# A transform kernel's first batch: folds on VectorE in a new order, half-rate samples as one narrow tile, masked copies a step ahead

## The chip, the cores and the metric

The kernel runs on one core of a Trainium2 chip. A core has TensorE (PE in the profile; PEld is its weight load), VectorE (DVE), ScalarE (ACT), GpSimd (POOL) and SyncE (SP, which only issues loads and stores here), each with its own stream of instructions, joined by semaphores. The metric is the device time of one execution in microseconds, as the median of several runs.

## What is computed

The input x is 4 x 3072 x 256. Three parts follow one another:

```python
X = np.fft.fft(np.fft.fft(x, axis=1), axis=2).real                     # attention
h = np.maximum(X @ w_in, 0.0); u, v = h[..., :512], h[..., 512:]       # moe
v_n = (v - mean(v)) / np.sqrt(var(v) + 1e-6)                           # over the last axis
v_s = np.einsum('ts,bsd->btd', w_spatial, v_n) + b_spatial[None, :, None]
y = (u * v_s) @ w_out
out = (sigmoid(y @ w_gate) * (y @ w_val)) @ w_out2                     # moe2, on 12288 rows
```

w_in is 256 x 1024, w_spatial 3072 x 3072. Where a product needs more than one pass's accuracy, a number is kept as a high and a low part (`h` and `l` at a name's end) and the product is three matmuls (`mm3`).

## The kernel before

The real part of the two-dimensional transform is symmetric, so that the sequence is folded (sums and differences of mirrored quarters, `folds`) before it is multiplied by cosine tables. A batch has three fold tiles `fo` (m = 0, 1, 2), each made from two half loads `xt` (`fold_x`, twelve two-input operations on a half), and split into `fh` and `fl` (`split_fold`; tile 2 first swaps some rows between partition halves by four ScalarE copies, `exchange`). The second axis, of 256, is folded into w_in: `first_weights` multiplies w_in, decoded from 64-bit words by `convert` into `wih` and `wil`, by `fd` into `gh`, `gl` and `g3`, once for all batches.

Two sets of samples stand outside of this scheme. The half-rate samples (column 128 of the 256, one value for a token and batch) are loaded as `xn`, three tiles of 128x1024, folded, split into `fohl` and multiplied by the same tables into `nts`; the copy `nt` of one unit is masked for one batch by ScalarE. The special samples `xs` (five slots of 128 columns) become `sps`, weighted by `spc` in some products.

The prologue makes all of this for batch 0 and the weights. It ends at about 70 us with the first `psv`. Then the main stage runs until about 346 us: 4 batches, each with four units (3, 2, 0, 1), each of eight or seven blocks: `v_block` (a product `psv` of 128 tokens by 512, of which half is mirrored: `ev`, `tv`) and `u_block` (`psu`, `eu`, `tu`). The order in which a block's parts are issued is written out by `put_off`: the first part in its step, the second (`second`, which reads the finished sum from its bank once by ScalarE and once by VectorE, `mirror`) `LAG` steps later, the third (relu and statistics, or the store) one step after that. Layer normalization of a unit (`ln1`, `root`, `ln2`, `norms`) follows some steps later. Folds and splits of the next batch are put into steps by a table (`plan`), on GpSimd. From 346 us on TensorE works through the products of w_spatial and what follows; nothing there is touched.

There is no scheduler: each engine does its instructions in the order in which the code issues them. Loads on SP's queue and on GpSimd's go out in their order on each; a load into a ring's buffer waits for the last reader of what was in it. The tables `c1`, `c2`, `c3`, `spc` and `fd` are loaded by GpSimd, the rest by SP.

Of the kernel before, what the change touches and what calls it, by code (L numbers as in the profile page):

```python
# [156 lines left out]
def layouts(x, moe_w_in, moe_w_spatial, moe_b_spatial, moe_w_out, moe2_w_gate, moe2_w_val, moe2_w_out):  # L157
# [14 lines left out]
    n = np.zeros((3, P, 8, P), np.float32)  # L172
    gn = g[..., D // 2].reshape(B, 3, P, 8)
    for b in range(B):
        for c in range(3):
            n[..., 32 * b + c] = gn[b]
# [3 lines left out]
    for at in (0, 32, 64):  # L180
# [9 lines left out]
        "xn": n,  # L190
# [48 lines left out]
def tile_kernel(ctx: ExitStack, tc: tile.TileContext, t: dict, out: bass.AP):  # L239
# [151 lines left out]
    def fft(fold, b, unit, q, e=0, ps=None):  # L391
# [49 lines left out]
    def convert(two):  # L441
        new = lambda: tmp.tile([P, 512], F32, tag="cv", name="cv", bufs=5)
        values = from64_rest(from64_first([words[i] for i in two], new), new())
        for i, value in zip(two, values):
            c, h = pieces[i]
            sl = slice(h * 512, h * 512 + 512)
            split(wih[0][:, c, sl], wih[1][:, c, sl], value)
# [9 lines left out]
    fold0(nc.vector, 0, 0)  # L457
    xts[2, 0] = load_x(0, 2, 0)
    fold0(nc.gpsimd, 1, 0)
    fd = tmp.tile([P, 2 * 512 + 256], F32R, name="fd")  # L460
    nc.gpsimd.dma_start(fd, t["fd"])
    fold0(nc.vector, 0, 1)
    words.append(load_w(2))
    xts[2, 1] = load_x(0, 2, 1)
    fold0(nc.gpsimd, 1, 1)
    load_table(cst, "c3", {"c3p": (3, R3), "c3q": (3, H)})
    nc.gpsimd.dma_start(spc, t["spc"])
    convert([0, 1])
    words.append(load_w(3))
    nc.sync.dma_start(masks, t["masks"])  # L470
    xs = tmp.tile([P, B + 1, 2, P], F32, name="xs")
    nc.sync.dma_start(xs, t["xs"])
    xns = []

    def load_xn(m):
        xn = tmp.tile([P, 8, P], F32, tag="xt", name="xn", bufs=RING)
        nc.sync.dma_start(xn, t["xn"][m])
        xns.append(xn)

    load_xn(0)  # L480
    load_xn(1)
    fold = [split_fold(fo[0], 0)]
    fold0(nc.vector, 2, 0)
# [12 lines left out]
    def first_weights(h):
# [8 lines left out]
        for a, ps in enumerate(sums):  # L505
            nc.scalar.copy(gc[0][:, a, sl], ps)
            nc.vector.tensor_tensor(out=gc[1][:, a, sl], in0=ps, in1=f(gc[0][:, a, sl]), op=ALU.subtract)
        ps = ps_w.tile([P, 512], F32, tag="pa", name="psg3")
        for c in range(2):
# [3 lines left out]
        nc.scalar.copy(g3[:, sl], ps)  # L513
        nc.vector.scalar_tensor_tensor(
            out=g3[:, sl], in0=f(g3[:, sl]), scalar=masks[:, 1:2], in1=ps, op0=ALU.mult, op1=ALU.add
        )

    first_weights(1)

    fold_n = []  # L520

    def fold_nyquist(eng, m):
        folds(eng, [(0, xns[m], xns[m][:, 4:8, :])])

    def split_nyquist(m):
# [18 lines left out]
    split_nyquist(2)
# [10 lines left out]

# [3 lines left out]
    up = pool(r0, "up", 3, "right")  # L559

    def unit_blocks(pq, b, unit):
# [20 lines left out]
        def v_block(m):  # L582
# [31 lines left out]
        def u_block(fb):  # L614
# [32 lines left out]
        def ln2():  # L647
# [709 lines left out]
```

## Time and profile before

| what | value |
|---|---|
| median of 3 runs | 2972.27 us (2971.44 to 2974.28) |
| the profiled execution | 2973.02 us, its span 2971.2 us |
| granted TensorE clock over the span | 0.990 |
| busy over the span | PE 2867.2, DVE 2064.7, ACT 1323.5, POOL 401.2 us |
| PE by 40 slices of 74 us, in tenths | 3 in the first, 8 in the next four, 9 in the rest |
| chain that ended last, share of the span | PE 87%, DVE 8%, ACT 2%, issue 2%, DMA 1% |
| q1 (SP) over the span | 143712 packets, 442.70 MB |
| q0 (GpSimd) over the span | 2320 packets, 14.82 MB |

Times of rows count from the start of the span. In a timeline row the first number is the start, the second the duration (of all of them, where a row ends in x2), and in brackets stands how long the engine was idle before it and what released it. Rows of one line and shape that follow one another are put together.

### The profile page before, as it was taken

How to read it: one execution, taken by the hardware profiler on the slowest of the kernel's cores; microseconds unless marked ns; L12 is line 12 of the kernel's file. 1: busy time of each engine (PE TensorE's matmuls, PEld its weight loads, DVE VectorE, ACT ScalarE, POOL GpSimd, SP SyncE). 2: the span in 40 equal slices, each digit the busy share in tenths (PEclk: the TensorE clock that was granted, in tenths of full speed). 3: DMA queues.
4: the chain of work that ended last, by engine and by line, in shares of the span. 5: the costliest groups of instructions: out<-in, count | busy, mean ns of one | idle time of the engine just before them, and what ended most of it. 6: DMA issues, size and time to landing. Idle time of an engine off the chain costs nothing.

```text
span 2971.2 us, 34046 instructions
## 1 busy us (share of the span) xinstructions
PE 2867.2 (96%) x12550; PEld 2359.4 (79%) x12550; DVE 2064.7 (69%) x2908; ACT 1323.5 (45%) x2117; POOL 401.2 (14%) x408
## 2 busy tenths in 40 slices
PE   3888899999999999999999999999999999999999
PEld 2777788888878888888887888788888888888887
DVE  8898875768765765576666476866666666766665
ACT  3777532323232232332223233655555555555554
POOL 5774121122111002111002010000000000000000
PEclk8999999999999999999999999999999999999999
DMA  6565875778765776776876474200000000000000
GB/s 230 187 235 221 313 276 196 278 244 316 264 221 175 260 252 211 242 257 222 282 259 223 154 271 166 84 29 29 29 10 20 29 29 29 15 15 29 29 15 15
DMA packets 149656, 472.28 MB, mean 159 GB/s; under 512 B 16624, under 2 KB 18160, under 8 KB 149104
## 3 DMA queue, kind: packets, MB, share of 16 engines
q1 hardware_dynamic: 143712, 442.70, 43.2%
q0 software_dynamic: 2320, 14.82, 1.3%
q10 hardware_dynamic: 3456, 12.58, 1.1%
q8 instruction: 98, 1.61, 0.2%
q14 instruction: 70, 0.57, 0.1%
HBM read 387.46 MB, written 82.58 MB: 158 GB/s over the span
## 4 chain that ended last, share of the span: by engine, by line
PE 87%; DVE 8%; ACT 2%; issue 2%; DMA 1%; ACTq 0%; DVEq 0%; SPq 0%
PE bank L261 28%; PE bank L262 28%; PE bank L260 28%; DVE stats L610 1%; DVE gl L994 1%; DVE g L986 1%; ACT wh L751 1%; DVE st L747 1%; DVE tv L580 0%; DVE wl L754 0%; DVE tu L580 0%; DMA v_d<-tv 0%; PE psv L588 0%; DVE tv L659 0%; PE psf L260 0%
## 5 line engine op out<-in xcount | busy, mean ns | idle before, releaser
L262 PE MATMUL bank<-wh,vl 128*128 128x512 f32 x2016 | 786.3, 390 | 0.0
L261 PE MATMUL bank<-wl,vh 128*128 128x512 f32 x2016 | 786.0, 390 | 0.0
L260 PE MATMUL bank<-wh,vh 128*128 128x512 f32 x2016 | 785.4, 390 | 0.0
L754 DVE TENSOR_TENSOR wl<-st,wh 128x1024 fp32r<-128x1024 f32 x252 | 331.4, 1315 | 390.9 <-ACT wh L751 388.9
L751 ACT CAST wh<-st 128x1024 fp32r<-128x1024 f32 x252 | 265.2, 1053 | 594.6 <-PE bank L262 351.6
L260 PEld LDWEIGHTS bank<-wh,vh 128*128 128x128 f32 x2016 | 379.3, 188 | 79.9
L261 PEld LDWEIGHTS bank<-wl,vh 128*128 128x128 f32 x2016 | 379.1, 188 | 80.0
L262 PEld LDWEIGHTS bank<-wh,vl 128*128 128x128 f32 x2016 | 378.9, 188 | 79.0
L1240 DVE TENSOR_TENSOR t<-t,bank 128x512 f32<-128x512 f32 x144 | 99.0, 688 | 250.3 <-PE bank L262 250.2
L747 POOL TENSOR_TENSOR st<-st 128x1024 f32<-128x1024 f32 x60 | 156.5, 2608 | 812.9 <-DMA st<-v_d 512.2
L261 PE MATMUL bank<-x,wgh 128*128 128x512 f32 x673 | 265.9, 395 | 0.0
L262 PE MATMUL bank<-x,wgl 128*128 128x512 f32 x673 | 265.5, 395 | 0.0
L260 PE MATMUL bank<-x,wgh 128*128 128x512 f32 x673 | 264.1, 392 | 0.4 <-ACT t L1252 0.4
L747 DVE TENSOR_TENSOR st<-st 128x1024 f32<-128x1024 f32 x180 | 226.1, 1256 | 53.9 <-DMA st<-in_wt 53.9
L1261 DVE TENSOR_TENSOR gl<-s,gh 128x512 fp32r<-128x512 f32 x288 | 199.4, 693 | 57.4 <-ACT gh L1259 44.5
L262 PE MATMUL bank<-gh,wv 128*128 128x512 f32 x576 | 227.6, 395 | 0.0
L260 PE MATMUL bank<-gh,wv 128*128 128x512 f32 x576 | 226.8, 394 | 0.8 <-ACT gh L1254 0.8
L261 PE MATMUL bank<-gl,wv 128*128 128x512 f32 x576 | 225.8, 392 | 0.2 <-DVE gl L1261 0.2
L1231 ACT ACTIVATE s<-s 128x512 f32<-128x512 f32 x144 | 91.0, 632 | 149.0 <-DVE s L1230 149.0
L260 PEld LDWEIGHTS bank<-x,wgh 128*128 128x128 f32 x673 | 126.4, 188 | 31.2 <-ACT t L1252 0.8
L261 PEld LDWEIGHTS bank<-x,wgh 128*128 128x128 f32 x673 | 126.3, 188 | 30.6
L262 PEld LDWEIGHTS bank<-x,wgl 128*128 128x128 f32 x673 | 126.2, 188 | 28.6
(233 smaller groups left out, 4564.2 us busy)
## 6 DMA issues: line engine op xcount, KB each, us to landing
st<-in_wt SPq DMA_DIRECT2D x432, 512.0 KB, 5.3
st<-v_d SPq DMA_DIRECT2D x144, 512.0 KB, 4.9
u<-u_d SPq DMA_DIRECT2D x96, 256.0 KB, 4.4
u_d<-tu SPq DMA_DIRECT2D x56, 384.0 KB, 3.1
v_d<-tv SPq DMA_DIRECT2D x80, 256.0 KB, 2.5
xt<-in_xh SPq DMA_DIRECT2D x24, 512.0 KB, 4.6
x_d<-x ACTq DMA_DIRECT2D x24, 512.0 KB, 3.2
raw<-x_d SPq DMA_DIRECT2D x24, 512.0 KB, 4.5
```

Of the source, the lines that this page charges most:

```text
L260: nc.tensor.matmul(out=ps, lhsT=w[0], rhs=x[0], start=first, stop=False, **kw)
L261: nc.tensor.matmul(out=ps, lhsT=w[0], rhs=x[1], start=False, stop=False, **kw)
L262: nc.tensor.matmul(out=ps, lhsT=w[1], rhs=x[0], start=False, stop=last, **kw)
L610: nc.vector.bn_stats(stats[:, sg * 3 + m, :], tiles[sg * 3 + m])
L747: (nc.gpsimd if kind == "v" else nc.vector).tensor_tensor(out=tiles[0], in0=tiles[0], in1=tiles[1], op=ALU.add if sign > 0 else ALU.subtract)
L751: nc.scalar.copy(hl[0], tiles[0])
L754: lows.append(lambda: nc.vector.tensor_tensor(out=hl[1], in0=tiles[0], in1=f(hl[0]), op=ALU.subtract))
L986: nc.vector.scalar_tensor_tensor(out=g, in0=side["u"][d], scalar=0.0, in1=g, op0=ALU.max, op1=ALU.mult)
L994: side["low"] = lambda: nc.vector.tensor_tensor(out=gl, in0=g, in1=f(gh), op=ALU.subtract)
L1231: nc.scalar.activation(s1, s1, AF.Sigmoid)
L1240: nc.vector.tensor_tensor(out=g["t2"], in0=g["t2"], in1=g["b"], op=ALU.add)
L1261: nc.vector.tensor_tensor(out=l, in0=s, in1=f(h), op=ALU.subtract)
```

## The change

Six things are different.

- All six half folds of batch 0 are on VectorE; three of them were on GpSimd. Conversion of the words, the `wil` halves, the folds and the weights' second parts are issued in a new order.
- The half-rate samples of all batches and tiles are one tile of 128 x 8 x 12, folded once on VectorE (48 columns and fewer) and spread to the places of `fohl`, three columns for a batch, when they are split; the rest of `fohl` is set to zero by GpSimd.
- GpSimd's loads of `c3`, `spc` and `c2` stand right after that of `fd`.
- The special samples are mirrored in two parts, two slots before the first product and three after the half-rate products.
- In the main stage VectorE's `mirror` is issued ahead of ScalarE's copy of the same bank, and the masked copy `nt` of the following unit is issued in the step of a unit's last block (`own_samples`).
- `ln2` has four operations on the root instead of five.

```diff
-    def fold0(eng, m, hd):
-        fold_x(eng, xts[m, hd], fo[m], hd, new_et(tmp if eng is nc.gpsimd else xp))
+    def fold0(m, hd):
+        fold_x(nc.vector, xts[m, hd], fo[m], hd, new_et())
 
     xts[0, 0] = load_x(0, 0, 0)
-    xts[1, 0] = load_x(0, 1, 0)
     xts[0, 1] = load_x(0, 0, 1, tmp, RING)
     words = [load_w(0), load_w(1)]
+    xts[1, 0] = load_x(0, 1, 0)
     xts[1, 1] = load_x(0, 1, 1, tmp, RING)
...
+    nc.sync.dma_start(masks, t["masks"])
+    xn = tmp.tile([P, 8, 3 * B], F32, name="xn")
+    nc.sync.dma_start(xn, t["xn"])
...
     load_table(cst, "c3", {"c3p": (3, R3), "c3q": (3, H)})
     nc.gpsimd.dma_start(spc, t["spc"])
...
+    fold0(0, 0)
+    fold0(0, 1)
+
+    fn = tmp.tile([P, 4, 3 * B], F32, name="fn")
+    folds(nc.vector, [(0, xn, fn)])
+    exchange(fn[:64, 1, 2 * B :], fn[64:, 0, 2 * B :])
+    xts[2, 0] = load_x(0, 2, 0)
+    xts[2, 1] = load_x(0, 2, 1, tmp, RING)
+    rest = convert([0, 1])
+    words += [load_w(2), load_w(3)]
     load_table(cst, "c2", {"c2p": (3, H), "c2q": (3, H)})
...
+    fold0(1, 0)
+    rest()
...
+    take = first_weights(1)
+    fold0(1, 1)
...
+    mirror_samples(slice(0, B + 1, B))
+    fold = [split_fold(fo[0], 0)]
+    take()
+    rest = convert([2, 3])
+    fold0(2, 0)
+    rest()
+    take = first_weights(0)
+    fold0(2, 1)
+    fold.append(split_fold(fo[1], 1))
...
+    for m in range(3):
         if m == 2:
-            exchange(xns[m][:64, 5, :], xns[m][64:, 4, :])
+            fold.append(split_fold(fo[2], 2))
         hl = fop.tile([P, 2, 4, P], F32R, tag="fo", name="fohl")
-        split(hl[:, 0], hl[:, 1], xns[m][:, 4:8, :])
+        nc.gpsimd.memset(f(hl), 0.0)
+        hi, lo = (hl[:, i].rearrange("p s (b k) -> p s b k", k=32)[:, :, :, 0:3] for i in range(2))
+        src = fn[:, :, m * B : m * B + B].unsqueeze(3).to_broadcast([P, 4, B, 3])
+        nc.scalar.copy(hi, src)
+        nc.vector.tensor_tensor(out=lo, in0=src, in1=f(hi), op=ALU.subtract)
         fold_n.append((hl[:, 0:1], hl[:, 1:2]))
...
+    mirror_samples(slice(1, B))
...
+    def own_samples(b, unit):
+        nt = stp.tile([P, R3], F32R, tag="nt", name="nt", bufs=1)[:, : R3 if unit == 3 else H]
+        nc.scalar.activation(nt, f(nts[unit]), AF.Identity, scale=masks[:, 3 + b : 4 + b])
+        nt_of[b, unit] = nt
...
+                mirror(tiles[3 + m], ev, ps)
                 nc.scalar.activation(tiles[m], ps, AF.Relu)
-                mirror(tiles[3 + m], ev, ps)
...
+                mirror(tu[:, 1, :], eu[:, :H], ps[:, :H])
                 nc.scalar.copy(tu[:, 0, :], ps[:, :H])
-                mirror(tu[:, 1, :], eu[:, :H], ps[:, :H])
...
-            nc.vector.tensor_tensor(out=sd[:, a], in0=y[:, a], in1=y[:, a], op=ALU.mult)
-            nc.vector.tensor_tensor(out=sd[:, a], in0=sd[:, a], in1=ve[:, a], op=ALU.mult)
-            nc.vector.tensor_scalar(out=sd[:, a], in0=sd[:, a], scalar1=-0.5, scalar2=1.5, op0=ALU.mult, op1=ALU.add)
-            nc.vector.tensor_tensor(out=y[:, a], in0=y[:, a], in1=sd[:, a], op=ALU.mult)
+            stt(out=ve[:, a], in0=y[:, a], scalar=-0.5, in1=ve[:, a], op0=ALU.mult, op1=ALU.mult)
+            nc.vector.tensor_tensor(out=ve[:, a], in0=ve[:, a], in1=y[:, a], op=ALU.mult)
+            stt(out=y[:, a], in0=ve[:, a], scalar=1.5, in1=y[:, a], op0=ALU.add, op1=ALU.mult)
...
-            put_off(step, block)
+            put_off(step, block, follows if block is blocks[-1] else None)
```

First place, the loads at the start. SP's queue before, from its first load (`xt` are the halves of batch 0, `words` those of w_in):

```order
L366 DMA xt<-in_xh 128x1024 x3
L265 DMA words<-in_w_in 128x1024 x2
L366 DMA xt<-in_xh 128x1024 x2
L265 DMA words<-in_w_in 128x1024
L366 DMA xt<-in_xh 128x1024
L265 DMA words<-in_w_in 128x1024
L470 DMA masks<-in_masks 128x7
L472 DMA xs<-in_xs 128x1280
L477 DMA xn<-in_xn 128x1024 x3
```

and now, up to the first loads of the next batch:

```order
L362 DMA xt<-in_xh 128x1024 x2
L261 DMA words<-in_w_in 128x1024 x2
L362 DMA xt<-in_xh 128x1024 x2
L467 DMA masks<-in_masks 128x7
L469 DMA xn<-in_xn 128x96
L471 DMA xs<-in_xs 128x1280
L362 DMA xt<-in_xh 128x1024 x2
L261 DMA words<-in_w_in 128x1024 x2
L362 DMA xt<-in_xh 128x1024 x3
```

GpSimd's stream now begins, after its constants, with four loads; of before it had twelve fold operations ahead of `fd`, twelve more ahead of `c3` and `spc`, and a third half ahead of `c2`:

```order
L466 DMA fd<-in_fd 128x1280
L326 DMA c_167<-in_c 128x4620
L473 DMA spc<-in_spc 128x1538
L326 DMA c_238<-in_c 128x4608
L544 MEMSET fohl 128x1024 [waits DVE_49] x3
L326 DMA c_434<-in_c 128x4608
```

`xn` is now one narrow load in the eighth place of SP's queue (two, two, two and the masks stand ahead), and 128x1280 to 128x4608 of tables are issued by GpSimd beside it; the memsets of `fohl` wait for VectorE.

Second place, ScalarE in the prologue, from its first instruction to the weights. Before:

```order
L276 ACT_TABLE_LOAD
L276 ACTIVATE cv<-words 128x512
L277 ACTIVATE cv<-words 128x512
L276 ACTIVATE cv<-words 128x512
L277 ACTIVATE cv<-words 128x512
L255 CAST wih<-cv 128x512 x2
L255 CAST fh<-fo 128x1024
L491 CAST sps<-es 128x5x128
L491 CAST sps<-xs 128x5x128
L506 CAST gh<-psg 128x512 x2
L513 CAST g_133<-psg_314 128x512
```

and now:

```order
L341 COPY ex<-fn 64x4
L342 COPY ex<-fn 64x4
L343 COPY fn<-ex 64x4
L344 COPY fn<-ex 64x4
L272 ACTIVATE cv<-words 128x512
L273 ACTIVATE cv<-words 128x512
L272 ACTIVATE cv<-words 128x512
L273 ACTIVATE cv<-words 128x512
L448 CAST wih<-cv 128x512 x2
L524 CAST sps<-es 128x2x128
L524 CAST sps<-xs 128x2x128
L251 CAST fh<-fo 128x1024
```

Four exchange copies of `fn`, which VectorE writes after the fold of `xn`, stand ahead of the first words, and the cast `fh` stands behind those of the samples.

Third place, ScalarE at the first change of units in the main stage (batch 0, from unit 3 to unit 2), with what each instruction waits for. Before:

```order
L622 COPY eu<-psu 128x386 [waits PE_49,Activation_49]
L628 COPY tu<-psu 128x384 [waits PE_49]
L608 ACTIVATE tv<-tv 128x512 [waits DVE_49]
L570 ACTIVATE nt<-nt_136,masks 128x384
L595 COPY ev<-psv 128x512 [waits PE_49]
L622 COPY eu<-psu 128x384 [waits PE_49,Activation_49]
L628 COPY tu<-psu 128x384 [waits DMAHW2_49,PE_49]
```

and now:

```order
L637 COPY eu<-psu 128x386 [waits PE_49,Activation_49]
L576 ACTIVATE nt<-nt_136,masks 128x384
L644 COPY tu<-psu 128x384 [waits DVE_49]
L623 ACTIVATE tv<-tv 128x512
L610 COPY ev<-psv 128x512 [waits PE_49]
L637 COPY eu<-psu 128x384 [waits PE_49,Activation_49]
L644 COPY tu<-psu 128x384 [waits DMAHW0_49,DVE_49]
```

`nt` of the next unit has moved ahead of `tu` and `tv`'s relu, and `tu`, which waited for TensorE, now waits for VectorE's `mirror`; VectorE's own wait on ScalarE at that place is gone, and its second statistic waits for the relu.

## Rows read from the trace of the kernel before

**Rows 1.** Windows of the main stage: start:end, length, busy time by engine, clock, DMA.
```profile
100.00:280.00 180.00, 151.95 (x722) 134.96 (x721) 163.75 (x368) 131.94 (x267) 124.14 (x180) 0.94 0.62 222
```

**Rows 2.** Waits of PE, 70 to 346 us: total, times, longest.
```profile
PE psv L588 <- ACT nt L570: 34.3, 16, 6.3
```

**Rows 3.** Waits of DVE, 70 to 346 us.
```profile
DVE tv L580 <- ACT tv L602: 19.0, 11, 3.4
DVE tu L580 <- ACT tu L628: 9.2, 13, 1.5
```

**Rows 4.** Timeline of DVE, 0 to 72 us: start, duration, operation, wait before.
```profile
4.63 0.69 DVE L371 TENSOR_TENSOR et<-xt 128x512 f32<-128x512 f32 x1 [4.63 <-DMA xt<-in_xh]
...
20.83 1.02 DVE L282 TENSOR_SCALAR cv<-cv 128x512 f32<-128x512 f32 x2
...
27.32 3.29 DVE L256 TENSOR_TENSOR wil<-cv,wih 128x512 fp32r<-128x512 f32 x2
...
32.20 1.21 DVE L371 TENSOR_TENSOR et<-xt 128x512 f32<-128x512 f32 x1
...
37.38 0.21 DVE L362 TENSOR_TENSOR fo<-xt 128x64 f32<-128x64 f32 x1
...
42.70 1.27 DVE L507 TENSOR_TENSOR gl<-psg,gh 128x512 fp32r<-128x512 f32 x2
...
44.56 1.34 DVE L282 TENSOR_SCALAR cv<-cv 128x512 f32<-128x512 f32 x2
...
52.42 1.29 DVE L256 TENSOR_TENSOR wil<-cv,wih 128x512 fp32r<-128x512 f32 x2
...
56.80 1.23 DVE L256 TENSOR_TENSOR fl<-fo,fh 128x1024 fp32r<-128x1024 f32 x1 [1.60 <-ACT fh L255]
...
60.40 1.53 DVE L354 TENSOR_TENSOR xn<-xn 128x512 f32<-128x512 f32 x1
...
63.90 0.28 DVE L362 TENSOR_TENSOR xn<-xn 128x128 f32<-128x128 f32 x1
...
64.70 1.02 DVE L422 TENSOR_TENSOR pl<-psf,ph 128x386 fp32r<-128x386 f32 x2
```

**Rows 5.** DMA, 26 to 31 us: packets, MB; by queue (q0 POOL, q1 SP).
```profile
DMA packets 177, 2.14 MB, mean 428 GB/s; under 512 B 6, under 2 KB 6, under 8 KB 77
...
q0 software_dynamic: 100, 1.85, 88.3%
q1 hardware_dynamic: 77, 0.29, 15.4%
```

**Rows 6.** Timeline of ACT, 0 to 75 us.
```profile
8.85 0.67 ACT L276 ACTIVATE cv<-words 128x512 f32<-128x512 f32 x1 [6.83 <-DMA words<-in_w_in]
...
54.37 0.41 ACT L346 COPY ex<-fo 64x256 f32<-64x256 f32 x1
...
55.72 1.05 ACT L255 CAST fh<-fo 128x1024 fp32r<-128x1024 f32 x1
```

**Rows 7.** Timeline of POOL, 128 to 140 us.
```profile
130.59 2.40 POOL L256 TENSOR_TENSOR fl<-fo,fh 128x1024 fp32r<-128x1024 f32 x1 [9.94 <-ACT fh L255]
```

**Rows 8.** Timeline of ACT and of DVE, 206 to 211 us.
```profile
207.48 0.48 ACT L628 COPY tu<-psu 128x384 f32<-128x384 f32 x1
207.86 0.64 ACT L608 ACTIVATE tv<-tv 128x512 f32<-128x512 f32 x1
...
209.08 0.54 DVE L580 SCALAR_TENSOR_TENSOR tu<-eu,psu 128x384 f32<-128x384 f32 x1
209.54 1.27 DVE L610 BATCH_NORM_STATS2 stats<-tv 128x6 f32<-128x512 f32 x2
```

**Rows 9.** Groups of DVE by line, 70 to 346 us: total, mean ns.
```profile
L652 DVE TENSOR_SCALAR sd<-sd 128x6 f32<-128x6 f32 (+1 forms) x15 | 4.2, 281 | 0.5
```

**Rows 10.** Timeline of ACT and of PE, 184 to 191 us.
```profile
187.80 0.81 ACT L663 ACTIVATE tv<-tv,nm,y 128x512 f32<-128x512 f32 x1 [2.33 <-DVE nm L654]
...
190.03 0.80 PE L588 MATMUL psv<-g,nt 128*128 128x512 f32 x1 [4.60 <-ACT nt L570]
```

More of the change, by code (lines that the diff above doesn't have):

```diff
@@ L171, in layouts @@
     xh = halves(g).reshape(B, 3, P, 8, 2, 2, 64).transpose(0, 1, 5, 2, 3, 4, 6)
[L172 to L176, printed above, removed]
+    gn = g[..., D // 2].reshape(B, 3, P, 8).transpose(2, 3, 1, 0)
     fam = np.array([384, 1152, 1920, 2688])
@@ L409, in fft @@
         for i, (m, s, c) in enumerate(ops):
+            if i not in tiles:
+                continue
             fh, fl = fold[m]
@@ L446, in convert, with rest @@
             sl = slice(h * 512, h * 512 + 512)
-            split(wih[0][:, c, sl], wih[1][:, c, sl], value)
-    def fold0(eng, m, hd):
-        fold_x(eng, xts[m, hd], fo[m], hd, new_et(tmp if eng is nc.gpsimd else xp))
+            hi, lo = (x[:, c, sl] for x in wih)
+            nc.scalar.copy(hi, value)
+            parts.append((hi, lo, value))
+        def rest():
+            for hi, lo, value in parts:
+                nc.vector.tensor_tensor(out=lo, in0=value, in1=f(hi), op=ALU.subtract)
@@ L463, in tile_kernel @@
[L463 to L465 removed]
+    nc.sync.dma_start(masks, t["masks"])
+    xn = tmp.tile([P, 8, 3 * B], F32, name="xn")
+    nc.sync.dma_start(xn, t["xn"])
+    xs = tmp.tile([P, B + 1, 2, P], F32, name="xs")
+    nc.sync.dma_start(xs, t["xs"])
     load_table(cst, "c3", {"c3p": (3, R3), "c3q": (3, H)})
     nc.gpsimd.dma_start(spc, t["spc"])
[L468 to L471, printed above, removed]
@@ L512, in first_weights, with take @@
                 nc.tensor.matmul(out=ps, lhsT=sign, rhs=wih[n][:, c, sl], start=c + n == 0, stop=c + n == 2)
[L513 to L518, printed above, removed]
+        def take():
+            for a, p in enumerate(sums):
+                nc.scalar.copy(gc[0][:, a, sl], p)
+            nc.scalar.copy(g3[:, sl], ps)
+            for a, p in enumerate(sums):
+                nc.vector.tensor_tensor(out=gc[1][:, a, sl], in0=p, in1=f(gc[0][:, a, sl]), op=ALU.subtract)
+            nc.vector.scalar_tensor_tensor(
+                out=g3[:, sl], in0=f(g3[:, sl]), scalar=masks[:, 1:2], in1=ps, op0=ALU.mult, op1=ALU.add
+            )
@@ new lines, in first_weights, with mirror_samples @@
+        return take
+    take = first_weights(1)
+    fold0(1, 1)
+    es = tmp.tile([P, B + 1, P], F32, name="es")
+    def mirror_samples(bs):
+        nc.vector.tensor_tensor(out=es[:, bs], in0=xs[:, bs, 0, :], in1=xs[:, bs, 1, :], op=ALU.add)
+        nc.vector.tensor_tensor(out=xs[:, bs, 1, :], in0=xs[:, bs, 0, :], in1=xs[:, bs, 1, :], op=ALU.subtract)
+        for q, e in ((0, es[:, bs]), (1, xs[:, bs, 1, :])):
+            nc.scalar.copy(sps[:, bs, q, :], e)
+            nc.vector.scalar_tensor_tensor(
+                out=sps[:, bs, q, :], in0=f(sps[:, bs, q, :]), scalar=masks[:, 2:3], in1=e, op0=ALU.mult, op1=ALU.add
+            )
@@ new lines, in tile_kernel @@
+        hi, lo = (hl[:, i].rearrange("p s (b k) -> p s b k", k=32)[:, :, :, 0:3] for i in range(2))
+        src = fn[:, :, m * B : m * B + B].unsqueeze(3).to_broadcast([P, 4, B, 3])
+        nc.scalar.copy(hi, src)
+        nc.vector.tensor_tensor(out=lo, in0=src, in1=f(hi), op=ALU.subtract)
+        fold_n.append((hl[:, 0:1], hl[:, 1:2]))
+    sums = [fft(fold, 0, 3, q, tiles=(0, 1)) for q in range(2)]
+    for q in range(2):
+        fft(fold, 0, 3, q, ps=sums[q][0], tiles=(2,))
+    take()
@@ L831, in tile_kernel, with put_off @@
     step = 0
-    def put_off(step, block=None):
+    def put_off(step, block=None, also=None):
         if block is not None:
             seconds[step + LAG] = block()
+            if also is not None:
+                own_samples(*also)
         if step in seconds:
```

60 lines of the change are left out of this document (11 added, 49 removed).

## The prediction

> **What bounds the kernel now.** I read the page's tenths first: TensorE is full nearly everywhere, but not in the first 346 us, and the diff touches nothing later. So I cut those 346 us into the prologue (to the first `psv`, about 70 us) and the main stage, and asked for windows of the latter. From 100 to 280 us VectorE is busy 163.75 of 180 us, TensorE 151.95, ScalarE 131.94, at a granted clock of 0.94 [rows 1]. VectorE has 16.2 us free there and is the nearest thing to a bound, with TensorE close behind.
>
> The list of waits says who stands still for whom from 70 to 346 us: TensorE waits 34.3 us in 16 places for ScalarE's `nt`, the copy of the samples that is masked for the batch [rows 2]; VectorE waits 19.0 us for the `tv` half and 9.2 us for the `tu` half that ScalarE reads first out of the same bank [rows 3].
>
> The prologue's timeline shows VectorE filled from 4.63 us to the end of `pl` (65.7 us); its one wait of over a microsecond before that, 1.60 us, is for the cast of `fh` [rows 4]. A two-input operation costs more while GpSimd folds beside it: the same pair of `wil` takes 3.29 us at 27.32 us and 1.29 us at 52.42 us. So whatever keeps VectorE from its prologue work moves the whole kernel by as much.
>
> **Loads.** All six half folds and the fold of the half-rate samples now run on VectorE, the latter right behind the first two halves. Their tile `xn` is one load of 128x96, eighth on SP's queue, behind six loads of 0.524 MB (3.15 MB, by 128x1024 four-byte elements) and the masks. GpSimd, which has no folds any more, issues `fd`, `c3`, `spc` and `c2` at once at the start: 128 x (1280 + 4620 + 1538 + 4608) x 4 bytes are 6.17 MB that used to be spread to about 37 us. How two queues share is seen between 26 and 31 us: together 428 GB/s, with 100 records and 1.85 MB on GpSimd's, 77 records and 0.29 MB on SP's [rows 5]. They take turns by records, and GpSimd's are 18.5 KB against 3.8. By partitions, its four loads have 512 records and SP's six 768, so all of GpSimd's bytes pass before SP's queue gets to `xn`: 3.15 + 6.17 = 9.32 MB. At 0.428 MB/us that is 21.8 us. The first load is usable at 4.63 us, of which its own 0.524 MB is 1.2; the rest, 3.4 us, I take as start and landing. `xn` is then usable at 25.2 us, and with the masks and 128 small records of its own at about 25.5.
>
> A half fold on a free VectorE is 2 x (0.69 + about 0.40 + 2 x 0.28 + 2 x 0.21) = 4.1 us (128x512, 128x128 and 128x64 at 4.63, 63.90 and 37.38 us in [rows 4]; the 0.40 of 128x256 is my estimate between 0.28 and 0.69), less overlaps of some 0.07 each, so between 3.3 and 4.1; I take 3.6. VectorE asks for `xn` at 4.63 + 0.3 (the first load shared) + 2 x 3.6 = 12.1, and waits until 25.5: **13.4 us**. The bounds are 0, if SP's six loads pass before GpSimd's start, and 7 more (21.8 / 3) if the rate is only three quarters of that in [rows 5]; I take 13.4, the value by the row.
>
> [...] The trace agrees with turns, but its 1.85 against 0.29 MB are no equal bytes; if they were equal, the second rival below would hold.
>
> **VectorE's prologue.** Removed or cheaper: three halves at 4.63 to 20.83 and 32.20 to 37.6 were 21.6 us, and six at 3.6 are 21.6: 0. First conversion's `wil` pair and `fl`, 27.32 to 32.20, 4.9 us, become 2 pieces of 0.64 and one of 1.23 [rows 4]: -2.4. Special samples, 37.6 to 42.70, 5.1 us for five slots; two of five now, 2.0: -3.1. Second conversion, 44.56 to 52.42, 7.9 us, against 6.5 for the first (20.83 to 27.32), which had less beside it: -1.4. The last half-rate fold with its `lo`, 60.40 to 64.70, and one earlier `lo` of 0.6: 4.9, now five operations of 48 columns and fewer and small `lo`, 7 x 0.2 by the row of 128x64: -3.5. Own wait at 56.80: -1.6. Sum **-12.0**.
>
> Added: 0.3 for the shared first load; 13.4 for `xn`; 2.8, since ScalarE now has four exchange copies of 64x4 ahead of the words' ACTIVATEs and these wait for VectorE's `fn`: four copies at 0.25 (0.41 for 64x256 in [rows 6]), and three of the four ACTIVATEs at 0.6, start to start (0.67 in [rows 6]). Before, they were done by 12 us, under the folds. 0.6 for the first `fl`: its cast `fh`, 1.05 us, is now queued behind the casts of the samples, and VectorE has one sample operation of some 0.5 to fill it with. At the end: the pad tile of the half-rate samples takes the buffer of `fo`, so GpSimd's memset waits for `fl` of tile 1, ScalarE's `hi` for the memset, and the exchange, `fh` and `fl` of tile 2 are queued behind it. No trace row shows a memset of 128x1024; the nearest on GpSimd is its two-input operation of that shape, 2.40 us [rows 7], the other bound is nearly nothing; I take 1.2, half. With `hi` 0.3, exchange 1.6 and `fh` 1.05 [rows 6] that is 4.1, of which 0.3 lies beside `lo`: 3.8. `gh` stands behind the next memset: 1.0. Sum **+21.9**, net **+9.9**, that is prologue later by 10.
>
> The other special samples (three of five slots) now stand between VectorE's masked `nt` and the first stage step; ScalarE's own `nt` for step 0 is queued behind their two casts: 3/5 of 5.1 is 3.1, partly beside TensorE's first product: **+2.0** (0 to 3.1).
>
> **Main stage.** The order in a pair changes: VectorE's `mirror` first, ScalarE's copy behind it. At 207.48 ScalarE copies `tu`, at 207.86 does the `relu` of `tv`, both done 0.6 us before VectorE mirrors at 209.08 and goes straight into two statistics of 0.64 at 209.54 [rows 8]. In the new order ScalarE's 0.38 (start to start) and 0.64 begin when the mirror ends, while the first statistic covers 0.60 of them; with 0.04 to hand over, the second waits 0.04 + 0.38 + 0.64 - 0.60, near 0.5; I take 0.55. There are 48 such pairs (three mirrored `v` blocks in each of 16 units), by 180 of 276 us about 31 between 100 and 280: +17. Against it stand VectorE's present waits of 28.2 us in [rows 3], of which little lies in the stretch that VectorE fills, since all its idle time there is 16.2: I give back 8. `ln2` loses an operation: the middle ones are 128x6 and one such line cost 4.2 us over 15 units [rows 9], on VectorE throughout: -4.2. The clock and smaller edits: 0, hidden under VectorE. Sum 17 - 8 - 4.2 = **+4.5** rounded; the bounds are -25 (all of VectorE's waits go, no new ones) and +17.
>
> `nt` one step ahead: at the boundary of two units TensorE waits 4.60 us at 190.03 for `nt`. But ScalarE had stood 2.33 us before a norm at 187.80 that waits for VectorE's `nm` [rows 10]. In the new order `nt` moves past one `tv` of 0.6 us and still comes behind that norm. So I give it 0.5 at each boundary, nearly all beside VectorE: 0.
>
> **Sum.** 9.9 + 2.0 + 4.5 = +16.4. The profiled execution took 2973.02 us (span 2971.2, 1.8 around it), 0.75 above the median of the runs, 2972.27. 2973.02 + 16.4 = 2989.4; by the median 2988.7. I say 2989.
>
> **Rivals.** (1) The loads aren't starved: GpSimd's descriptors come late, `xn` passes early and the 13.4 fall away: 2989 - 13.4 = 2976. For it: the four loads have to be written by GpSimd first; against it: six SP loads alone need 7.4 us, and GpSimd is idle meanwhile. [...]
>
> (2) The queues share by bytes: `xn` comes when both have moved 3.15 MB, 6.3 / 0.428 = 14.7 + 3.4 = 18.1 us, the wait is 6.2, and the time 2989 - 7.2 = 2982.
>
> (3) Faster: the masked copies ahead work. If the boundaries where TensorE waits for `nt` go, 34.3 us of [rows 2], TensorE's stage gains some 25 of them; it decides if VectorE has room for it, and between 100 and 280 us it has 16.2. Then 2973 + 12 - 25 = 2960. Against it: [rows 10], where `nt` stays behind the norm.
>
> (4) Both starving and the swap at their upper ends: over 3000.
>
> **Chances.** Forecast 0.57 (own range 2979 to 3000), (1) 0.16, (2) 0.09, (3) 0.13, (4) 0.05. The range 2964 to 3000 leaves out half of (3) and (4) and some of the forecast's edges. What a measurement of this kernel tells from no change is 0.2%, 5.9 us: 2966 to 2978. Faster: nearly all of (3), 0.12. Same: (1), and the forecast's lowest edge, 0.2. Slower: 0.68.
>
> **What would show it.** In the trace after: a VectorE wait of some 13 us before the fold of `xn`, ended by DMA; first `psv` near 82 us instead of 70; second statistics waiting about 0.5 us for ScalarE; `psv` waits for `nt` of about the same 30 us. I am wrong if `xn` lands by 13 us, if the stage from the first `psv` to the last `nm` is over 10 us shorter, or if `nt` waits shrink to a third.

## The result, and the profile after

The changed kernel takes 3007.8 us (median of 4 runs, 3005.03 to 3008.53) against 2973.28 us (4 runs): 34.5 us slower, ratio 1.0115 with a 95% interval of 1.0097 to 1.0132. That is the forecast side, but above the range. The prologue came out near what was worked out, and the main stage much longer.

The simplest cut is the first and the last start of the product `psv<-g,nt`, which TensorE does 52 times in the main stage. Of before:

```profile
L588 PE MATMUL psv<-g,nt x52: 389/397/797, 71.5 to 337.9; 128*128 128x512 f32 x52
```

and of the changed kernel:

```profile
L603 PE MATMUL psv<-g,nt x52: 389/397/797, 84.0 to 372.1; 128*128 128x512 f32 x52
```

The first start moved from 71.5 to 84.0 us (+12.5, where 9.9 + 2.0 = 11.9 were forecast). From the first to the last, 266.4 us became 288.1: **+21.7, where +4.5 were forecast.** Behind the last start 2633.3 us became 2634.1.

The prologue first. VectorE's timeline after (start, duration, operation, wait), to be held against [rows 4]:

```profile
4.58 0.69 DVE L367 TENSOR_TENSOR et<-xt 128x512 f32<-128x512 f32 x1 [4.58 <-DMA xt<-in_xh]
...
7.93 0.68 DVE L367 TENSOR_TENSOR et<-xt 128x512 f32<-128x512 f32 x1
...
11.15 0.22 DVE L358 TENSOR_TENSOR fo<-xt 128x64 f32<-128x64 f32 x1
26.42 0.21 DVE L350 TENSOR_TENSOR xn<-xn 128x48 f32<-128x48 f32 x1 [15.05 <-DMA xn<-in_xn]
...
28.42 0.43 DVE L278 TENSOR_SCALAR cv<-cv 128x512 f32<-128x512 f32 x1 [1.06 <-ACT cv L272]
...
67.74 1.22 DVE L252 TENSOR_TENSOR fl<-fo,fh 128x1024 fp32r<-128x1024 f32 x1 [2.56 <-ACT fh L251]
...
73.68 1.01 DVE L420 TENSOR_TENSOR pl<-psf,ph 128x386 fp32r<-128x386 f32 x2
```

Two half folds at 3.35 us each (4.58 to 7.93), and then a wait of 15.05 us for `xn`, usable at 26.4 us (25.5 forecast). The DMA queues between 10 and 20 us say why, as in [rows 5]:

```profile
DMA packets 572, 4.14 MB, mean 414 GB/s; under 512 B 64, under 2 KB 64, under 8 KB 447
...
q0 software_dynamic: 285, 3.10, 75.3%
q1 hardware_dynamic: 287, 1.04, 28.4%
```

285 records on GpSimd's queue stand against 287 on SP's, but 3.10 MB against 1.04: equal numbers of records, of 10.9 and of 3.6 KB. Equal bytes it was not, so that this rival is out. Turns by records, as the forecast had them, fit these counts; how many records make a turn, the counts don't show. The rival by late descriptors is out as well: by 6 us GpSimd's queue had 74 records through, beside SP's 305.

The rest of the prologue came near the sum: the last `fl`, which waits 2.56 us for its cast, starts at 67.74 us, where it stood at 56.80, and `pl` at 73.68 where it stood at 64.70 [rows 4]. That is 9.0 us later (9.9 forecast); from there to the first `psv` another 3.5 us came in (2.0 forecast, 3.1 at most), so that two misses partly cancel. The memset of 128x1024, which no row showed before, takes 0.95 us on GpSimd (1.2 assumed). GpSimd's second memset, and TensorE's first `psv`:

```profile
63.72 0.95 POOL L544 MEMSET fohl<- 128x1024 f32 x1 [16.01 <-DVE fl L252]
```

```profile
84.05 0.50 PE L603 MATMUL psv<-g,nt 128*128 128x512 f32 x1 [3.44 <-ACT nt L576]
```

Now the main stage. The same stretch of time, 100 to 280 us, now begins 12.5 us earlier in the stage; still, VectorE is busy much less there, 141.88 us, where it was 163.75 [rows 1].

```profile
100.00:280.00 180.00, 147.28 (x667) 130.08 (x666) 141.88 (x315) 112.80 (x234) 130.33 (x203) 0.91 0.56 201
```

The waits of VectorE from 83 to 378 us (total, times, longest), in place of [rows 3]:

```profile
DVE stats L625 <- ACT tv L623: 24.7, 46, 1.5
DVE stats L625 <- ACT tv L618: 8.8, 6, 2.6
DVE pl L420 <- ACT ph L419: 8.7, 7, 4.0
DVE tv L595 <- PE psv L258: 7.7, 6, 4.7
DVE tu L595 <- PE psu L258: 2.3, 6, 0.7
```

The waits of ScalarE and of TensorE there; `nt` answers to [rows 2]:

```profile
ACT tu L644 <- DVE tu L595: 62.6, 51, 3.4
ACT tv L618 <- DVE tv L595: 23.9, 33, 1.5
```

```profile
PE psv L603 <- ACT nt L576: 32.5, 10, 6.5
PE psv L256 <- ACT ev L610: 14.7, 11, 2.0
```

Before (70 to 346 us), the last of these rows, and ScalarE's one wait for a mirror, that of the relu of `tv`:

```profile
PE psv L260 <- ACT ev L595: 0.4, 1, 0.4
ACT tv L608 <- DVE tv L580: 2.1, 4, 0.8
```

The statistics, which waited for nothing, now wait 33.5 us in 52 places; the mirrors' 28.2 us for ScalarE are down to 2.1 (for `eu` and `ev`), but 10.0 us for TensorE have come (7.7 and 2.3); ScalarE, which waited 2.1 us for the mirrors, waits 86.5; and TensorE, which waited 0.4 us for `ev`, waits 14.7. One pair, ScalarE and VectorE, against [rows 8]:

```profile
127.35 0.48 ACT L644 COPY tu<-psu 128x384 f32<-128x384 f32 x1 [2.28 <-DVE tu L595]
127.73 0.63 ACT L623 ACTIVATE tv<-tv 128x512 f32<-128x512 f32 x1
```

```profile
126.78 0.54 DVE L595 SCALAR_TENSOR_TENSOR tu<-eu,psu 128x384 f32<-128x384 f32 x1
127.24 0.68 DVE L625 BATCH_NORM_STATS2 stats<-tv 128x6 f32<-128x512 f32 x1
128.39 0.69 DVE L625 BATCH_NORM_STATS2 stats<-tv 128x6 f32<-128x512 f32 x1 [0.47 <-ACT tv L623]
```

The mirror of `tu` ends at 127.3, ScalarE's copy starts then, its relu 0.38 behind it and 0.63 long; the first statistic is through at 127.9 and the second waits 0.47 us. The forecast had 0.55 a pair, and the 46 waits of this kind, 24.7 us, are 0.54 each. So the wait was seen rightly, one by one; what the new order does to the stage was not. The 2.28 us that ScalarE stands before its copy of `tu` had no term in the forecast.

### The profile page after: what moved, and what is told of

It reads as the page before. It is cut to its first block, busy times and chain, and to the rows that moved or that the text cites. A ratio compares the mean times of both kernels' runs of the same rounds, so it can differ in the third digit from the quotient of the medians.

```text
span 3006.2 us, 33971 instructions
## 1 busy us (share of the span) xinstructions
PE 2878.8 (96%) x12550; PEld 2366.9 (79%) x12550; DVE 2061.2 (69%) x2932; ACT 1318.0 (44%) x2119; POOL 367.1 (12%) x365
## 4 chain that ended last, share of the span: by engine, by line
PE 86%; DVE 7%; ACT 3%; issue 2%; DMA 1%; POOL 0%; SPq 0%; DVEq 0%; ACTq 0%; POOLq 0%
PE bank L258 28%; PE bank L257 28%; PE bank L256 27%; DVE st L762 1%; DVE g L1004 1%; DVE gl L1012 1%; ACT tv L623 1%; DVE tv L674 1%; DMA xt<-in_xh 1%; DVE tu L595 1%; ACT wh L766 0%; PE psf L256 0%; DMA words<-in_w_in 0%; DVE wl L769 0%; PE psf L257 0%
## 5 line engine op out<-in xcount | busy, mean ns | idle before, releaser
L256 PEld LDWEIGHTS bank<-x,wgh 128*128 128x128 f32 x673 | 126.4, 188 | 31.2 <-ACT t L1270 0.8
```

Of the source, the lines that this page charges most:

```text
L256: nc.tensor.matmul(out=ps, lhsT=w[0], rhs=x[0], start=first, stop=False, **kw)
```

## The experiments

Each was timed in three rounds beside the kernel before, whose median in the four sessions was 2972.95, 2971.73, 2971.85 and 2973.96 us; a ratio stands to that of its session. All lengths of the main stage are first to last start of `psv<-g,nt` in a profiled execution, which may lie some 5 us from the median.

**e1, copy first.** In the changed kernel, both pairs of lines turned back:

```diff
-                mirror(tiles[3 + m], ev, ps)
                 nc.scalar.activation(tiles[m], ps, AF.Relu)
+                mirror(tiles[3 + m], ev, ps)
...
-                mirror(tu[:, 1, :], eu[:, :H], ps[:, :H])
                 nc.scalar.copy(tu[:, 0, :], ps[:, :H])
+                mirror(tu[:, 1, :], eu[:, :H], ps[:, :H])
```

> The changed kernel, with ScalarE's copy of the bank again ahead of VectorE's mirror in both places; the masked copies stay a step ahead. Theory (the swapped order costs the main stage some 20 of its 21.7 us, since the second statistic now waits 0.5 us for a relu that is queued behind the copy): the time falls from 3008 to 2986-2991, the statistics' waits for the relu (25 us) are gone, and the main stage is back at 266-268 us. Rival (the stage is longer because it starts with later loads, or because the masked copies moved): 3000 or more.

2976.76 us, ratio 1.0015 (1.0005 to 1.0024); main stage 260.4 us. The swapped order is 31 of the 34.5 us, more than the 20 expected, and 27.7 us of the main stage; with it gone the stage is 6 us shorter than before: something else in the change is a gain. The mean granted clock over the span is 0.989 in e1's profiled execution and 0.988 in the changed kernel's; a thousandth of the span is 3 us (an estimate), so that little of the swap's price is the clock's.

**e2, tables late.**

```diff
+    seen = tmp.tile([P, 1], F32, name="seen")
+    nc.gpsimd.tensor_copy(seen, xn[:, 7, 0:1])
     load_table(cst, "c3", {"c3p": (3, R3), "c3q": (3, H)})
```

> The changed kernel, but GpSimd reads one column of the half-rate samples before it issues c3, spc and c2, so that these tables go out after the samples have landed. Theory (VectorE's 15 us wait for the samples comes from 5.4 MB of tables that pass ahead of them): samples usable at 11-12 us, the wait is gone, first psv at 69-71 us instead of 84, the time falls by 13-15 us to 2993-2995. Rival (the samples wait for SP's own six loads, or the late tables then hold up the first product): the first psv moves by less than 5 us, and the time stays above 3002.

2994.2 us, 13.6 less; ratio 1.0073 (1.0058 to 1.0088). First `psv` at 71.7 us, main stage unchanged at 288.6. The term of the loads is confirmed in place and size. The wait for `xn` is down to 2.67 us (read in e3, whose prologue is the same).

**e3, both edits.**

> Both edits: copy first and tables late. If the two costs are independent, 3008 - 20 - 14 = 2972 to 2976, no better than the kernel before to within 0.2%. If the masked copies ahead, the shorter root and the quieter prologue are worth something by themselves, below 2968.

2964.95 us, ratio 0.9975 (0.9965 to 0.9986), clear of no change: the remaining parts of the change are worth 7 to 8 us.

**e4, the swap alone,** in the kernel before, the same two pairs of lines.

> The kernel before with nothing changed but VectorE's mirror ahead of ScalarE's copy in both places. Theory (the swap by itself lengthens the main stage): 2990-2995, with 20-25 us of waits of the second statistic for the relu. Rival (the swap alone does nothing, it hurts only with the masked copies ahead of it on ScalarE): 2970-2976.

3012.8 us, ratio 1.0134 (1.0119 to 1.0149): +39.9, twice what the theory had; main stage 305.5 us. Its waits, of VectorE, ScalarE and TensorE:

```profile
DVE stats L610 <- ACT tv L608: 25.0, 48, 1.5
DVE tu L580 <- PE psu L262: 18.6, 16, 2.1
DVE tv L580 <- PE psv L262: 8.6, 10, 2.9
```

```profile
ACT tu L629 <- DVE tu L580: 61.0, 51, 3.8
ACT tv L603 <- DVE tv L580: 32.3, 36, 1.7
```

```profile
PE psv L588 <- ACT nt L570: 55.9, 16, 8.2
```

The mirrors wait 6.8 us for ScalarE (for `ev` and `eu`) in place of the 28.2 of [rows 3], and 27.2 us for TensorE, which in turn waits 55.9 us for `nt`, not 34.3.

**e5, relu first,** in the changed kernel:

```diff
+        if step in thirds:
+            thirds.pop(step)()
         if step in seconds:
             thirds[step + 1] = seconds.pop(step)()
-        if step in thirds:
-            thirds.pop(step)()
```

> The changed kernel, mirror still ahead of the copy, but in every step the third part of the earlier block (ScalarE's relu and VectorE's two statistics, or the store) is issued ahead of the second part of the next one, so that the relu no longer stands behind the copy that waits for the mirror. Theory A (the swap costs by the statistic that waits in line for the relu, 25 us over 47 pairs, and by what VectorE then does late): these waits go, the main stage falls from 288 to 262-268 us, the time to 2982-2988. Theory B (the swap costs because ScalarE's copies now run behind VectorE, so that its ev, even and nt come late for TensorE): waits for the relu go, but the stage stays above 278 us and the time above 2998.

3007.15 us, ratio 1.0116 (1.0101 to 1.0131); main stage 284.0. It told nothing apart: the waits of the statistics did not go, they fell from 33.5 to 25.2 us, 10.8 of these now for the other half, since the statistics stand earlier too. Time and stage are where theory B had them, but its condition, that these waits go, was not met.

**e6 and e7, the swap for one of the two,** with tables late. e6 has VectorE first for `tu` alone, e7 for `tv` alone.

> Tables late, and the order swapped for tu alone (62 places); tv has the copy first again. Compared with both edits at 2965 and tables late alone at 2994. Theory A: the relu stands behind the tu copy, so nearly the whole price is here: 2986-2994, statistics waiting 24-26 us for the relu. Theory B: each swap costs by its share of the places where ScalarE runs behind: about 62 of 110, so 2978-2984.

3028.23 us, ratio 1.0184 (1.0167 to 1.0201): 63 us more than e3 and 34 more than with both swapped, outside both expectations. The statistics wait less than with both swapped, 19.5 us against 33.0, and the price of the swap is twice as large: their waits alone are not the price.

> Tables late, and the order swapped for tv alone (48 places); tu has the copy first again. Theory A: next to nothing, 2962-2970; or a gain, since VectorE no longer waits for the tv copy (21 us in 13 places with both edits). Theory B: 2974-2982.

2976.18 us, ratio 1.0012 (1.0003 to 1.0022): 11 more than e3, without any wait of a statistic: within theory B's range and above theory A's. In e6 the two engines wait crosswise:

```profile
136.84 0.48 ACT L646 COPY tu<-psu 128x384 f32<-128x384 f32 x1 [1.76 <-DVE tu L597]
...
140.06 0.58 ACT L612 COPY ev<-psv 128x512 f32<-128x512 f32 x1
140.53 0.60 ACT L619 ACTIVATE tv<-psv 128x512 f32<-128x512 f32 x1
```

```profile
136.26 0.55 DVE L597 SCALAR_TENSOR_TENSOR tu<-eu,psu 128x384 f32<-128x384 f32 x1
141.17 0.69 DVE L597 SCALAR_TENSOR_TENSOR tv<-ev,psv 128x512 f32<-128x512 f32 x1 [4.36 <-ACT tv L619]
```

ScalarE stands 1.76 us before its `tu` until VectorE has mirrored; the exchange and `fh` of the next batch, `ev` and the `tv` copy queue behind it; and VectorE, done at 136.8, waits 4.36 us for that `tv`. Of all the waits of VectorE in e6 this kind is the largest:

```profile
DVE tv L597 <- ACT tv L619: 57.5, 45, 5.7
```

**e8, masked copies ahead, alone.** `own_samples` and its call in `put_off`, put into the kernel before.

> The kernel before with nothing but the masked copy of the following unit moved to the step of a unit's last block. With the copy first the whole change shortened the main stage by 5 to 6 us (266.4 to 260.4 and 261.5), by this and by the root's operation less. As predicted for this part (0, it stays behind the norm): 2971-2975, TensorE's waits for nt at 32 us or more. Rival (the masked copies are the gain): 2965-2969.

2964.02 us, ratio 0.9974 (0.9965 to 0.9983); main stage 259.5 us. The rival is right (the time is 1 us below its range): this is a gain of 8 us, as much as e3 has.

```profile
PE psv L593 <- ACT nt L565: 28.4, 8, 6.9
```

```profile
DVE tv L585 <- ACT tv L607: 17.7, 12, 3.4
...
DVE tu L585 <- ACT tu L633: 3.8, 8, 1.2
```

The waits for `nt` fall from 16 to 8. Four long ones stay, as the forecast said of those behind a norm, and grow from 20.3 to 25.2 us together; that of [rows 10], by which it judged them all, is one of these four. Eight others, of 0.9 to 2.0 us each and some 12 us together, are gone.

**e9, the `tu` copy a step later.** `tv` with the copy first; `tu`:

```diff
                 mirror(tu[:, 1, :], eu[:, :H], ps[:, :H])
-                nc.scalar.copy(tu[:, 0, :], ps[:, :H])
...
+                def rest():
+                    nc.scalar.copy(tu[:, 0, :], ps[:, :H])
+                    queue.dma_start(at, tu.rearrange("p a k -> p (a k)"))
```

> Tables late, tv with the copy first, tu with VectorE's mirror first, but ScalarE's tu copy put off to the block's third part, one step behind the mirror, with the store. Against 3028, where the same copy stands right behind the mirror. Theory B (ScalarE is held in line behind VectorE, and with it what TensorE needs next): ScalarE finds the mirror done, its 115 us of waits fall below 25, the main stage goes from 318 to 258-268 us, the time to 2962-2972. Rival (the mirror first is bad for VectorE itself, as it then waits for TensorE): above 2985.

2975.99 us, ratio 1.0013 (1.0003 to 1.0023); main stage 263.8 us against 317.9 in e6. ScalarE's waits for the mirrors fall from 113.6 to 17.3 us. A little above the expectation; the copy now holds its bank a step longer (TensorE waits 6.3 us for it). But no statistic waits either, so it tells the theories no further apart. It shows what the crossing in e6 costs: with nothing changed but the place of that copy, 52 us go.

**e10, copy first and a prologue without its waits.** Beside the two edits above: `xn` third on SP's queue, GpSimd's tables behind the sixth load, the exchange of `fn` behind `rest = convert([0, 1])`, and before the half-rate parts:

```diff
     fold.append(split_fold(fo[1], 1))
+    take()
+    fold.append(split_fold(fo[2], 2))
```

> The changed kernel with the copy first again and a prologue without the waits that the traces showed: the narrow half-rate load third on SP's queue, GpSimd's tables behind the last of the first six loads, the exchange of the half-rate fold behind the first conversion, the second weights' take and the exchange of tile 2 ahead of the half-rate samples' parts. Against 2965 with both edits: its waits of 2.7, 1.7, 1.2 and 2.6 us on VectorE go, first psv at 64-67 us instead of 71.7, 2957-2961. If the prologue is no longer bound by VectorE there: 2963-2967.

2957.73 us, ratio 0.9954 (0.9939 to 0.9968): the fastest, 14 us below the kernel before. First `psv` at 65.7 us, main stage 258.1.

```profile
65.71 0.50 PE L604 MATMUL psv<-g,nt 128*128 128x512 f32 x1 [3.44 <-ACT nt L577]
```

**e11, the root's four operations, alone.**

> The kernel before with nothing but the root's four operations instead of five. As predicted (on VectorE's path throughout): -4, 2968. Rival (hidden, since with the masked copies alone the main stage was already as short as with both): 2971-2974.

2972.69 us, ratio 1.0002 (0.9992 to 1.0011): nothing, where the forecast had -4.2.

**e12, no reading of the bank by VectorE.**

```diff
-                mirror(tu[:, 1, :], eu[:, :H], ps[:, :H])
+                mirror(tu[:, 1, :], eu[:, :H], eu[:, :H])
```

(the same for `tv`).

> The kernel before, with mirror reading ScalarE's copy of the first sum twice instead of that copy and the bank: it leaves out the second sum in the mirrored half. ScalarE and VectorE then no longer wait for one another at the bank. It prices the waits that the predicted sum counted: if VectorE's 28 us there were on the path, 2945-2960; if they cost nothing (VectorE has that much slack, as TensorE waits for nt behind the norm anyway), 2968-2975.

2986.63 us, ratio 1.0051 (1.0036 to 1.0066): outside both, and no price of the waits, since the mirrors themselves grew (before, then e12):

```profile
L580 DVE SCALAR_TENSOR_TENSOR tu<-eu,psu 128x384 f32<-128x384 f32 x62 | 33.9, 546 | 9.5 <-ACT tu L628 9.2
L580 DVE SCALAR_TENSOR_TENSOR tv<-ev,psv 128x512 f32<-128x512 f32 x48 | 32.5, 678 | 21.9 <-ACT tv L602 19.0 <-DMA v_d<-tv 2.6
```

```profile
L580 DVE SCALAR_TENSOR_TENSOR tu<-eu 128x384 f32<-128x384 f32 x62 | 42.8, 690 | 1.1 <-DMA u_d<-tu 1.1
L580 DVE SCALAR_TENSOR_TENSOR tv<-ev 128x512 f32<-128x512 f32 x47 | 42.1, 895 | 4.9 <-DMA v_d<-tv 3.8 <-ACT ev L595 1.1
```

The mirrors take 18.5 us more of VectorE, and the main stage went from 266.4 to 282.9. Their waits for ScalarE's copy of the bank are gone (1.1 us is left, for `ev`), so these come with VectorE's reading of the bank. But the statistics now wait 13.8 us, and TensorE 45.6 us for `nt` instead of 34.3, so that e12 gives neither the price of the waits nor that of VectorE's time by itself.

**e13 and e14, statistics a step later,** tables late; e13 with the mirror first, e14 with the copy first.

```diff
-                for sg in range(2):
-                    nc.vector.bn_stats(stats[:, sg * 3 + m, :], tiles[sg * 3 + m])
+                def count():
+                    for sg in range(2):
+                        nc.vector.bn_stats(stats[:, sg * 3 + m, :], tiles[sg * 3 + m])
+                return count
```

> Tables late, mirror ahead of the copy in both places as in the changed kernel, but VectorE's two statistics of a pair are issued one step later than ScalarE's relu of it, so that they find it done. Against 2994 with the statistics in the relu's step. Theory A (the price of the swap is the statistics' waits, 34 us): these go and the time falls to 2963-2972. Theory B (the price is that ScalarE's copies stand in line behind VectorE's mirror, 90 us of waits, and ev, eu and nt come late for TensorE): the statistics' waits go below 5 us, ScalarE's waits for the mirror stay above 70 us, and the time stays above 2983.

> The control of the last: statistics a step later, copy first, tables late. If that move by itself is neutral: 2962-2968, as with both edits (2965). If it delays the norms, and so the units, it is slower by some us, and the last run is to be compared with this one.

e13 2973.57 us, ratio 1.0000 (0.9990 to 1.0010), 1.6 us above theory A's range and 9 below theory B's; e14 2980.89, 1.0024 (1.0015 to 1.0033), so that the move is not neutral by itself. In e13 the waits of VectorE's statistics, ScalarE's for the mirror, and TensorE's largest:

```profile
DVE stats L629 <- ACT tv L625: 2.0, 4, 0.6
```

```profile
ACT tu L650 <- DVE tu L597: 54.3, 48, 3.4
...
ACT tv L620 <- DVE tv L597: 8.8, 13, 1.5
```

```profile
PE psv L605 <- ACT nt L578: 21.7, 9, 5.6
```

ScalarE still waits over 60 us for the mirrors, yet the swap now costs nothing: e13 is 7 us faster than its control, where with the statistics in their old place the swap costs 29 (e2 against e3). So ScalarE's waits by themselves, theory B's cause, are not the price. Nor are the statistics' waits by themselves, theory A's: e7 pays 11 us without any, and e6 twice the price with fewer. The waits that theory B named for TensorE went down in e13 too, those for `nt` from 30.3 us in e2 to 21.7 and those for `ev` from 13.9 to 3.5.

What the costly runs (the changed kernel, e2, e4, e5, e6) share is a crossing of two waits. ScalarE's copy waits for VectorE's mirror, and VectorE then waits for that copy or for something behind it in ScalarE's queue: a statistic for the copy or the relu, in e6 above all the next mirror for the `tv` copy. Taking the crossing away on either side took the price away, on VectorE's by e13 (29 us down to -7, each against its own control), on ScalarE's by e9 for `tu` alone (63 us above e3 down to 11). e13 is not as fast as e3 (8 to 9 us above); the statistics a step later cost by themselves (e14, some 15 us above e3, with 40 us of mirrors waiting for ScalarE).

Put together: VectorE's waits in the pairs, added up from each trace's list of waits (statistics for ScalarE, mirrors for ScalarE, mirrors for TensorE), beside the main stage. e12 is left out, as its mirrors have other lengths.

| run | statistics | mirror for ScalarE | mirror for TensorE | sum | main stage | ScalarE for mirrors |
|---|---|---|---|---|---|---|
| e8 | 0 | 21.5 | 0 | 21.5 | 259.5 | 2.8 |
| e10 | 0 | 22.1 | 0 | 22.1 | 258.1 | 2.2 |
| e9 | 0 | 22.7 | 2.1 | 24.8 | 263.8 | 17.3 |
| e3 | 0 | 25.1 | 0 | 25.1 | 261.5 | 2.2 |
| e1 | 0 | 25.4 | 0 | 25.4 | 260.4 | 2.2 |
| e13 | 2.0 | 6.0 | 17.6 | 25.6 | 265.2 | 61.6 |
| before | 0 | 28.2 | 0 | 28.2 | 266.4 | 2.1 |
| e11 | 0 | 30.0 | 0 | 30.0 | 268.0 | 2.6 |
| e7 | 0 | 25.0 | 11.8 | 36.8 | 271.1 | 53.4 |
| e5 | 25.2 | 0 | 13.1 | 38.3 | 284.0 | 87.8 |
| e14 | 0 | 40.0 | 0 | 40.0 | 268.6 | 1.1 |
| e2 | 33.0 | 1.5 | 10.8 | 45.3 | 288.6 | 88.2 |
| after | 33.5 | 2.1 | 10.0 | 45.6 | 288.1 | 86.5 |
| e4 | 31.2 | 6.8 | 27.2 | 65.2 | 305.5 | 91.0 |
| e6 | 19.5 | 57.5 | 0 | 77.0 | 317.9 | 113.6 |

The main stage goes roughly with the sum: from before to e4 +37.0 and +39.1, from e3 to e6 +51.9 and +56.4, from before to e8 -6.7 and -6.9, but from e1 to the changed kernel +20.2 and +27.7, and from e3 to e14 +14.9 and +7.1. In good part this is arithmetic: VectorE's work in the stage is nearly the same in these runs (226.7 us busy before, 221.4 in the changed kernel; the stage less all listed waits of VectorE is 220 to 230 us in all of them, 237 in e6), so a longer stage must show as more idle time of VectorE. The table says where that time lies; it doesn't say what caused it, which only the experiments above can. e5 and e14 fit worst, 15 us apart at nearly the same sum: outside of the pairs VectorE waits 26.1 us in e5 (11.2 before `pl` and 11.4 before `even`, both for the next units' transforms) and 7.6 in e14. ScalarE's waits alone don't order the runs (e13).

## Why the prediction was wrong

Between the two profiled executions lie 35.0 us. The prologue has 12.5 of them (11.9 forecast), the swapped order 27.7 (17 - 8 = 9 forecast; by e1), the rest of the main stage -6.0 (`ln2` and `nt`, -4.2 forecast), and 0.8 lie behind it. The forecast's sum of the stage, 17 - 8 - 4.2, is 4.8 and not 4.5, which changes nothing here.

**Loads: right.** A wait of 13.4 us was forecast and 15.05 measured; taken away, it gave back 13.6 us (e2) or 11.8 (e1 against e3).

**VectorE's prologue and the tail: right as a sum.** 11.9 forecast for the first `psv`, 12.5 measured, with some luck in the parts: 9.0 instead of 9.9 up to `pl`, 3.5 instead of 2.0 behind it. A half fold took 3.35 us, not 3.6, which makes up for most of the 1.65 us by which the wait for `xn` was longer.

**Main stage, the step that failed: the term of the swapped order.** Its 17 - 8 = +9 measured +27.7 in the main stage of the changed kernel, 31 of its time (e1), and +39.9 alone (e4). "The second waits 0.04 + 0.38 + 0.64 - 0.60, near 0.5; I take 0.55" was right by the pair. What was wrong is what it was summed to, in three places. It counted some 31 pairs, those in the stretch that VectorE fills, and treated the others as free; 46 such waits came, and six of another kind, for the half that ScalarE reads from the bank (8.8 us), 33.5 us together. "I give back 8" for the mirrors' waits on ScalarE: nearly all of the 28.2 us went, but 10.0 us of waits for TensorE came in their place (27.2 in e4, where 21.4 of the 28.2 went). And ScalarE's own wait had no term. By [rows 8] ScalarE is 2.1 us ahead there, from its copy's start at 207.48 to the mirror's end at 209.62; the new order takes this lead away, for the copy and for all that stands behind it: 86.5 us of waits, with TensorE's for `ev` at 14.7 us instead of 0.4. e13 and e9 show that this costs where VectorE next needs what stands behind that copy.

The idle time of [rows 1], 16.2 us, was read as room, by which the give-back was cut to 8; the swap alone cost more than twice as much. That VectorE, late by its statistics, is late with the norms, these hold up ScalarE's `nt`, and TensorE then the next sum, is how I read the lists of e4; the chain was not tested link by link.

None of the signs of being wrong in the forecast came up, and all four that were to show it right did (a DMA wait before `xn`, the first `psv` some 12 us later, statistics waiting half a microsecond, waits for `nt` about the same). They looked at single waits, and for a main stage that is shorter; none would have shown that it is longer.

**`ln2`: wrong,** -4.2 against nothing in e11. In e11 the lines from `ve` to `nm`, 65 to 350 us, take 31.2 us of VectorE instead of 33.0: the operation is gone, but those left are longer (`ve` 612 ns instead of 509, `nm` 298 instead of 242). And VectorE's waits are 30.0 us instead of 28.2. The mean of 0.28 us in [rows 9] is made by a few long ones: of the 16 of that line the shortest takes 0.170 us, the median one 0.172, the longest 1.22. The five that take 0.25 us or more have an operation of GpSimd beside them in the trace, the other eleven none. I now read these as waits beside GpSimd, which the next operation takes over; that was not tested.

**`nt` one step ahead: wrong,** 0 against -8 (e8). The argument held for the four long waits, of which [rows 10] shows one, and for these alone.

**The rivals.** The loads were starved (first and second out). The third, the faster side, was named rightly as mechanism and is worth 8 us, not 25; beside the swap and the starved load it did not show. The fourth gave the time, but not the way: the swap alone went beyond its upper end, the loads did not.

## What to carry to other kernels

Two engines read the same bank in turn here, and the one issued second waited: VectorE 28.2 us with the copy first (before), ScalarE 86.5 us with the mirror first (the changed kernel). So look at what stands in each one's queue behind it, above all whether the first one soon needs something that the second has queued behind its own reading (e6, where VectorE waits 57.5 us for the `tv` copy; e13, where its statistics, a step later, wait 2.0 us and not 33.0). Here the idle time of an engine that alternates with two others, 16.2 us of 180 by [rows 1], was no slack (e4: 39.9 us more): price a new wait for every place where it arises, and on both engines. A sum of waits that grows with a stage doesn't show their cause; moving one operation does (e13 and its control e14). In this prologue a narrow load that was needed at once belonged ahead of the bulk on its own queue, and bulk on the other queue behind it (e2, 13.6 us less; e10, where `xn` is used at 10.75 us without a wait): between 10 and 20 us of the changed kernel the two queues moved 285 and 287 records, but 3.10 and 1.04 MB.

## What the runs showed that was not expected

In the main stage, where GpSimd folds beside it, the mirror with both operands in SBUF is slower than with one in the bank: 690 against 546 ns for 128x384, 895 against 678 ns for 128x512 (e12 against before). GpSimd's own folds took longer as well: 957 and 970 instead of 835 and 810 ns for its two operations of 128x256.

GpSimd's queue and SP's moved equal numbers of records to within 1% between 10 and 20 us of the changed kernel (285 and 287), at 10.9 and 3.6 KB on average.

A half fold on VectorE takes 3.35 us with no operation of GpSimd's beside it (the changed kernel, 4.58 to 7.93 us), where the same twelve operations took 7.9 and 8.3 us while GpSimd folded (before, 4.63 to 20.83 us).
